# The output layer of a fused attention and feed-forward kernel: block products with w_out stationary and results turned by VectorE

## The chip, the core and the metric

The kernel runs on one core of a Trainium2 chip. A core has TensorE (PE in the profile; its weight loads are a row of their own, PEld), VectorE (DVE), ScalarE (ACT), GpSimd (POOL) and SyncE (SP), which here only issues DMAs. Each engine works through its own instructions in program order; semaphores make one wait for another. The metric is the device time of one execution in microseconds (us). The kernel before takes 675.25 us, the median of three runs (673.92 to 676.24).

## What is computed

Attention with two sparse masks (half of the heads look at the last 32 positions, half at every 32nd position before), and on its output a feed-forward layer: the maximum of three projections, and an output projection.

```
attn = softmax(mask(q @ k.T / 8)) @ v            # 8 batches, 8 heads, 576 positions, 64 wide
x = attn.transpose(0, 2, 1, 3).reshape(4608, 512)
h = maximum(maximum(x @ w1, x @ w2), x @ w3)      # 4608 x 768
out = h @ w_out                                   # 4608 x 512, float32
```

Every float32 operand of the feed-forward layer is kept as two parts, high and low, in the type float32r. A product is three matmuls: high by high, high by low, low by high.

## The kernel before

The 4608 tokens are worked in three sorts of pieces. Chunk one and chunk two are 512 tokens each; their products are plain ones (`ff_in`, L516; `ff_out`, L548). The 3584 tokens from 1024 on are eight blocks of 448, worked two at a time: four super-blocks of 896 tokens (`supers`, L773).

In a super-block the first layer is done by nine quads (L810), one for each pair of hidden blocks j, j+1 (128 features each) and each of w1, w2, w3. A quad computes a 2 x 2 block product (two hidden blocks by two token blocks, the inner dimension in two halves) by seven products instead of eight. They are named A11, S1, S2, S4, S3, A12, A22, in this order; each is a sum or difference of blocks of the weights by a sum or difference of blocks of x. The weights' sums are built once, while chunk two runs (`build_sums` to `build_low`, L577 to L616, on POOL), go to a scratch buffer in HBM, and are streamed back, one piece of 256 KB for each product, by SP (`load_next`, L664); nine buffers, so eight pieces ahead. The sums of x are made by `conversion` (L673) in seven steps for the next super-block, on ACT (high parts) and DVE (low parts and differences).

Two PSUM banks, `f_ps`, hold the products of a quad; one quad's first and second product take them in turn, and `bank` (L508) swaps the two at each call. ACT copies each product to SBUF (`snap`, L824), POOL adds earlier ones to it, and DVE takes the maximum into `hall` (L840), which holds h of the super-block: 768 features on partitions and blocks, by 896 tokens.

After nine quads follows the output layer of the super-block (L890 to L903): seven tiles of 128 tokens. `split` (L859) makes high and low parts of h for a tile; in `out_part` (L866) they are the stationary operand, and w_out (768 x 512, high and low, held in SBUF) is the moving one, 512 columns wide: 18 matmuls for a tile, 126 in all. `store` (L877) copies the tile to SBUF and stores it from ACT's queue. The seven steps of the next block's conversion stand between the tiles.

Attention of later batches runs in between, in pieces hung on the product numbers (`before`, `after`, L784 to L808); the last super-block has none. Everything is pinned to program order on its engine (`pin`, L100).

In chunk two, 18 groups `ff_in` (i = 0 to 17) are followed by four `ff_out` (L722 on). `ff_max` (L529) empties each bank: ACT for every third group, DVE for the other two, and at the end of three ACT and POOL make hh and hl, the parts of h. POOL builds the sums of w1, w2, w3 there at the places `sums_at` (L719).

## Time and profile before

| | us |
|---|---|
| median of three runs | 675.25 |
| lowest and highest | 673.92, 676.24 |
| span of the profiled execution, first to last instruction | 671.9 |
| TensorE busy | 647.1 |
| VectorE, ScalarE, GpSimd busy | 370.8, 336.5, 299.4 |
| chunk two, 126 to 193 us | 67 |
| the four output stages, each | 28.6 |

The profile gives the span of its execution and no other time for it. Busy times are shares of an engine's own time; they say nothing about who waits for whom, for which there are the chain that ended last and the rows of waits. The PE row counts pipelined matmuls: the time of one in a steady stretch is the stretch divided by the count, and its own duration (368 ns at 448 columns) is longer than that.

### The profile page before, as it was taken

What the parts mean: (1) busy time and instruction counts of PE and PEld (TensorE: products, weight loads), DVE (VectorE), ACT (ScalarE), POOL (GpSimd) and SP (SyncE); (2) the same over time, 40 slices, a digit from 0 to 9 for tenths busy, and PEclk for the clock granted to TensorE, in tenths of its full rate; (3) what the DMA queues carried; (4) which work ended last, traced back from release to release, by engine and by line L of the source; (5) the groups of instructions that cost most, each with busy time, mean ns of one, the idle gap of its engine ahead of it and who ended that gap; (6) DMA issues with size and microseconds to landing.
All of it is one profiled execution on the core that took longest, in us unless ns stands there. A gap on an engine that the chain in (4) does not pass through costs nothing.

```text
span 671.9 us, 18032 instructions
## 1 busy us (share of the span) xinstructions
PE 647.1 (96%) x7408; PEld 553.5 (82%) x7408; DVE 370.8 (55%) x515; ACT 336.5 (50%) x702; POOL 299.4 (45%) x291
## 2 busy tenths in 40 slices
PE   4689999999999999999999999999999999999997
PEld 3467877777778888888888888888899988999986
DVE  5886964676675666476345665643652563224240
ACT  4777656444264445446355455544444554444441
POOL 8779998599942233240134243004334401444410
PEclk9789999999999999999999999999999999999999
DMA  9999974567699777771377899228767714777411
GB/s 297 265 246 366 296 248 133 178 189 233 188 284 326 251 240 257 259 248 63 114 251 236 243 262 276 87 87 213 233 179 216 206 63 124 214 217 216 123 47 63
DMA packets 89371, 138.36 MB, mean 206 GB/s; under 512 B 10153, under 2 KB 39593, under 8 KB 89289
## 3 DMA queue, kind: packets, MB, share of 16 engines
q1 hardware_dynamic: 85256, 129.86, 63.6%
q10 hardware_dynamic: 4032, 7.34, 2.9%
q8 instruction: 59, 0.97, 0.6%
q14 instruction: 24, 0.19, 0.1%
HBM read 111.21 MB, written 25.95 MB: 204 GB/s over the span
## 4 chain that ended last, share of the span: by engine, by line
PE 80%; POOL 9%; DMA 6%; ACT 1%; DVE 1%; issue 1%; SPq 1%; POOLq 0%; ACTq 0%; DVEq 0%
PE f_ps L779 46%; PE f_ps L873 17%; PE f_ps L525 6%; PE f_ps L555 4%; DMA w<-in_w 4%; POOL work L596 2%; PE o_ps L444 2%; POOL work L612 2%; PE s_ps L318 2%; POOL work L588 2%; PE o_ps L473 1%; PE s_ps L340 1%; DMA out<-work 1%; POOL hl L546 1%; POOL sums_low L596 1%; DMA v_t<-in_v_loc 1%
## 5 line engine op out<-in xcount | busy, mean ns | idle before, releaser
L779 PE MATMUL f_ps<-xc,w_stream 128*128 128x448 f32 x1512 | 317.5, 368 | 0.2 <-ACT snap L826 0.2
L779 PEld LDWEIGHTS f_ps<-xc,w_stream 128*128 128x128 f32 x1512 | 280.5, 188 | 26.5 <-ACT snap L826 2.6
L826 ACT COPY snap<-f_ps 128x448 f32<-128x448 f32 x240 | 127.9, 533 | 165.0 <-PE f_ps L779 162.8
L838 POOL TENSOR_TENSOR snap<-snap 128x448 f32<-128x448 f32 x72 | 89.1, 1243 | 148.3 <-ACT snap L826 115.5
L840 DVE TENSOR_TENSOR h_all<-h_all,snap 128x448 f32<-128x448 f32 x96 | 81.2, 887 | 128.9 <-POOL snap L838 128.9
L838 POOL TENSOR_TENSOR h_all<-snap 128x448 f32<-128x448 f32 x36 | 41.4, 1150 | 169.1 <-ACT snap L826 168.1
L873 PE MATMUL f_ps<-wNone,h_parts 128*128 128x512 f32 x504 | 115.0, 389 | 0.0
L873 PEld LDWEIGHTS f_ps<-wNone,h_parts 128*128 128x128 f32 x504 | 94.6, 188 | 19.5
L525 PE MATMUL f_ps<-xh,w 128*128 128x512 f32 x288 | 95.8, 402 | 0.0
L525 PEld LDWEIGHTS f_ps<-xh,w 128*128 128x128 f32 x288 | 54.7, 190 | 12.7 <-ACT xh L498 0.3
L525 PE MATMUL f_ps<-xl,w 128*128 128x512 f32 x144 | 56.7, 394 | 0.8 <-DVE xl L503 0.8
L864 DVE TENSOR_TENSOR h_parts<-h_all,h_parts 128x768 fp32r<-128x768 f32 (+2 forms) x40 | 27.2, 712 | 30.3 <-ACT h_parts L863 30.1
L879 ACT COPY work<-f_ps 128x512 f32<-128x512 f32 x28 | 16.4, 585 | 46.1 <-PE f_ps L873 46.1
L683 DVE TENSOR_TENSOR xc<-x_block,xc 128x896 fp32r<-128x896 f32 x28 | 29.8, 1086 | 11.1 <-ACT xc L680 11.1
L397 DVE TENSOR_REDUCE s_ps<-s_ps 128x10 f32<-128x640 f32 (+2 forms) x30 | 23.2, 772 | 20.3 <-ACT s_ps L386 20.3
L407 DVE STREAM_TRANSPOSE pt<-s_ps 128x640 f32<-128x640 f32 (+2 forms) x32 | 32.5, 1017 | 1.1
L525 PEld LDWEIGHTS f_ps<-xl,w 128*128 128x128 f32 x144 | 27.4, 190 | 6.2 <-DVE xl L503 1.1
L555 PE MATMUL f_ps<-wNone,hh 128*128 128x512 f32 x96 | 30.6, 400 | 0.3 <-issue 0.3
L863 ACT CAST h_parts<-h_all 128x768 fp32r<-128x768 f32 (+2 forms) x40 | 24.5, 642 | 12.0 <-DVE h_all L840 5.4
L386 ACT ACTIVATE s_ps<-s_ps 128x640 f32<-128x640 f32 (+2 forms) x30 | 19.5, 651 | 21.9 <-DVE s_ps L370 21.9
L340 PEld LDWEIGHTS s_ps<-qk_t 64*32 64x32 f32 x1408 | 16.5, 116 | 15.2 <-DMA qk_t<-in_qT 7.0
L680 ACT CAST xc<-x_block 128x896 fp32r<-128x896 f32 x28 | 25.8, 947 | 3.4 <-DVE xc L683 1.2
(87 smaller groups left out, 681.6 us busy)
## 6 DMA issues: line engine op xcount, KB each, us to landing
w_stream<-scratch SPq DMA_DIRECT2D x252, 256.0 KB, 3.5
w<-in_w SPq DMA_DIRECT2D x18, 512.0 KB
qk_t<-in_qT SPq DMA_DIRECT2D x28, 288.0 KB, 3.8
qk_t<-in_kT SPq DMA_DIRECT2D x28, 288.0 KB, 5.9
v_t<-in_v_str SPq DMA_DIRECT2D x56, 128.0 KB, 4.2
out<-work ACTq DMA_DIRECT2D x28, 256.0 KB, 2.0
scratch<-w SPq DMA_DIRECT2D x27, 256.0 KB, 3.3
v_t<-in_v_loc SPq DMA_DIRECT2D x48, 96.0 KB, 3.3
```

What stands on the lines that cost most here:

```text
L407: pin(nc.vector.transpose(pt[:, :, : nm * at], s_ps[:, :, : nm * at]))
L525: pin(nc.tensor.matmul(f_ps, w[:, kc, :], x[:, kc, :], start=(kc == 2 and n == 0), stop=(kc == 1 and n == 2)))
L555: pin(nc.tensor.matmul(f_ps, h[:, ts], w, start=(j == 0 and n == 0), stop=(j == NJ - 1 and n == 2)))
L680: pin(nc.scalar.copy(out=x[m][:, 0], in_=src))
L683: pin(nc.vector.tensor_tensor(out=x[m][:, 1], in0=src, in1=x[m][:, 0].bitcast(F32), op=ALU.subtract))
L779: pin(nc.tensor.matmul(out_, w[:, wl, fs], x[:, xl, k, :], start=start and k == 0 and n == 0, stop=k == 1 and n == 2, skip_group_check=not ...
L826: pin(nc.scalar.copy(out=t, in_=src))
L838: pin(nc.gpsimd.tensor_tensor(out=h if i == 0 else u, in0=u, in1=t, op=ALU.add))
L840: pin(nc.vector.tensor_tensor(out=h, in0=h, in1=u, op=ALU.max))
L863: pin(nc.scalar.copy(out=to[:, 0, j0:j1], in_=src))
L864: pin(nc.vector.tensor_tensor(out=to[:, 1, j0:j1], in0=src, in1=to[:, 0, j0:j1].bitcast(F32), op=ALU.subtract))
L873: pin(nc.tensor.matmul(outs[t], h, w, start=(j == 0 and n == 0), stop=(j == NJ - 1 and n == 2)))
```

## The change

The output layer of a super-block becomes a 2 x 2 block product as well, with seven products instead of eight. w_out is now the stationary operand and h, 448 tokens wide, the moving one; the result comes out turned, features on partitions, and DVE turns it back in blocks of 32 by 32. The inner dimension, 768, is split by even and odd hidden blocks, so each product has three steps r of 128, in two halves q of 128 output features: 18 matmuls, 126 in all.

- The sums of w_out are built in chunk two, at i = 6 to 14, by DVE (`out_sums`, `out_mix`, and the low parts in `out_split`), stored to a second scratch buffer, and streamed in the place of w_out held in SBUF: 84 pieces for a super-block instead of 63.
- The columns of w_out are kept in another order (`by_quarters`), so that the blocks of 32 by 32 land in rows of 128 features; the plain chunks' outputs are put back in order by ACT's copy.
- The sums of h are made in place in `hall`: for r = 0 and 1 in the middle of the quads (`early`, at products 24 to 34 and 45 to 55), for r = 2 at the beginning of the output stage.
- In the output stage, sums of products are taken by POOL (`added`), turned by DVE (`turned`), and stored from SP's queue by four DMAs for 448 tokens, in pieces of 512 bytes.
- The first two steps of the next conversion move into the last quad (products 59 and 61); the others stand between the products of the output stage, and five of their DVE operations go to POOL there (`helper`).

The core of the diff:

```diff
+    def out_sums(r):
+        a = sums_o[r] = wt.tile([P, 2, 512], F32, name=f"w{r}_0")
+        for n in range(2):
+            parts = kept[None, 2 * r + n].bitcast(F32)
+            pin(nc.vector.tensor_tensor(out=a[:, n], in0=parts[:, 0], in1=parts[:, 1], op=ALU.add))
+
+    def out_mix(r):
+        a = sums_o[r]
+        a11, a21, a12, a22 = a[:, 0, :256], a[:, 0, 256:], a[:, 1, :256], a[:, 1, 256:]
+        for out_, x, y, op in (
+            (a22, a21, a22, ALU.add), (a21, a11, a21, ALU.subtract), (a11, a22, a11, ALU.subtract), (a12, a12, a11, ALU.subtract)
+        ):
+            pin(nc.vector.tensor_tensor(out=out_, in0=x, in1=y, op=op))
+
+    def out_split(r):
+        a, sh = sums_o.pop(r), wt.tile([P, 2, 512], F32R, name=f"w{r}_1")
+        to = scratch_o[:, :, r].rearrange("p n (l f) -> p n l f", l=2)
+        for n, (first, second_) in enumerate(((S2, S3), (S4, S1))):
+            pin(nc.scalar.copy(out=sh[:, n], in_=a[:, n]))
+            pin(nc.vector.tensor_tensor(out=a[:, n].bitcast(F32R), in0=a[:, n], in1=sh[:, n].bitcast(F32), op=ALU.subtract))
+            for l, src in enumerate((sh[:, n].bitcast(F32), a[:, n])):
+                pin(nc.sync.dma_start(out=to[:, first : second_ + 1 : 2, l], in_=halves(src)))
...
-    def conversion(s):
+    def conversion(s, helper=nc.vector):
...
         high(A11, b11)
-        high(A12, b21)
         low(A11, b11)
-        low(A12, b21)
         yield
         less(b11, b12, b11)
         yield
+        high(A12, b21)
+        low(A12, b21, helper)
         high(S4, b22)
+        low(S4, b22)
+        yield
+        less(b12, b22, b12, helper)
         high(S1, b11)
-        low(S4, b22)
-        less(b12, b22, b12)
+        low(S1, b11)
         yield
         less(b22, b22, b11)
-        low(S1, b11)
         high(S3, b12)
+        low(S3, b12, helper)
         yield
         high(S2, b22)
-        low(S3, b12)
-        less(b21, b21, b22)
+        less(b21, b21, b22, helper)
+        low(S2, b22)
         yield
         high(A22, b21)
-        low(S2, b22)
-        low(A22, b21)
+        low(A22, b21, helper)
...
+    out_at = {6 + 3 * r + n: (r, n) for r in range(NKO) for n in range(3)}
...
+        def h_high(m, rs):
+            if m not in parts:
+                parts[m] = second["hc"].tile([P, 2, NKO, BL], F32R, name="h_parts")
+            pin(nc.scalar.copy(out=parts[m][:, 0, rs], in_=of[m][:, rs]))
+        def h_low(m, rs, engine=nc.vector):
+            to = parts[m]
+            pin(engine.tensor_tensor(out=to[:, 1, rs], in0=of[m][:, rs], in1=to[:, 0, rs].bitcast(F32), op=ALU.subtract))
+        def h_split(m, rs):
+            h_high(m, rs)
+            h_low(m, rs)
+        def h_less(to, a, b, rs, engine=nc.vector):
+            pin(engine.tensor_tensor(out=to[:, rs], in0=a[:, rs], in1=b[:, rs], op=ALU.subtract))
+        def early(rs):
+            return [
+                lambda: h_split(A11, rs),
+                lambda: h_less(h11, h12, h11, rs),
+                lambda: (h_less(h12, h22, h12, rs, nc.gpsimd), h_split(S1, rs)),
+                lambda: h_less(h11, h22, h11, rs),
+                lambda: h_split(S2, rs),
+                lambda: h_less(h11, h21, h11, rs, nc.gpsimd),
+            ]
+        def out_stage(s):
+            more = lambda n=1: [next(convert[0], None) for _ in range(n)]
+            a0 = bank()[:, :BL]
+            c0 = ps_f[1 - turn[0]][:, :BL]
+            acc = {m: (a0, o[:, 0, :BL]) for m in (A11, S2, S3, A22)}
+            acc.update({m: (c0, o[:, 1, :BL]) for m in (S1, S4, A12)})
...
+                        for n, (wl, hl) in enumerate(((0, 0), (0, 1), (1, 0))):
+                            pin(nc.tensor.matmul(
+                                acc[m][q], w[:, wl, q * P : (q + 1) * P], parts[m][:, hl, r],
...
+            def turned(src, t, half_, q):
+                pin(nc.vector.transpose(outs[t][:, :, half_, q], src.rearrange("p (b r) -> p b r", r=32)))
+            def added(m, q, t, half_, u):
+                v = snap(acc[m][q])
+                pin(nc.gpsimd.tensor_tensor(out=v, in0=v, in1=u, op=ALU.add))
+                return lambda: turned(v, t, half_, q)
+            def store(t):
+                r0 = PLAIN + 2 * BL * s + (t - 1) * BL
+                for a in range(4):
+                    pin(nc.sync.dma_start(
+                        out=out[r0 : r0 + BL, a * P : (a + 1) * P].rearrange("(b r) n -> r b n", r=32),
+                        in_=outs[t][32 * a : 32 * (a + 1)].rearrange("p b h q f -> p b (h q f)"),
+                    ))
+            last, two, all_ = slice(2, 3), (0, 1), (0, 1, 2)
+            everything = slice(0, 3)
+            h_split(A11, last)
+            h_less(h11, h12, h11, last)
+            times(A11, two)
+            times(S1, two)
+            h_split(S1, last)
+            h_less(h12, h22, h12, last, nc.gpsimd)
+            h_less(h11, h22, h11, last)
+            h_split(S2, last)
+            times(A11, (2,))
+            s1 = [snap(acc[A11][q]) for q in range(2)]
+            h_less(h11, h21, h11, last, nc.gpsimd)
+            times(S1, (2,))
+            more()
+            h_split(S4, everything)
+            s5 = [snap(acc[S1][q]) for q in range(2)]
+            more()
+            times(S2, all_)
+            h_split(S3, everything)
...
+            times(S4, all_)
+            h_split(A12, everything)
+            w = [added(S4, 0, 2, 0, s2[0])]
+            more()
+            w.append(added(S4, 1, 2, 0, s2[1]))
+            times(S3, all_)
+            h_split(A22, everything)
+            w[0]()
+            v = [added(S3, 0, 2, 1, s5[0])]
+            more()
+            w[1]()
+            v.append(added(S3, 1, 2, 1, s5[1]))
+            times(A12, all_)
+            v[0]()
+            w = [added(A12, 0, 1, 0, s1[0])]
+            more()
+            v[1]()
+            store(2)
+            w.append(added(A12, 1, 1, 0, s1[1]))
+            times(A22, all_)
+            w[0]()
+            more()
+            turned(acc[A22][0], 1, 1, 0)
+            w[1]()
+            more()
+            turned(acc[A22][1], 1, 1, 1)
+            store(1)
+            more(20)
...
         for s in range(NSUPER):
+            convert[:] = [conversion(s + 1, nc.gpsimd) if s + 1 < NSUPER else iter(())]
+            between[59] = between[61] = [lambda: next(convert[0], None)]
+            for r, at in ((0, 24), (1, 45)):
+                for n, step in enumerate(early(slice(r, r + 1))):
+                    between[at + 2 * n] = [step]
             for q in range(9):
                 quad(s, q)
...
+            out_stage(s)
```

The three buffers of `h_parts` (the pool `hc`) serve the seven products in turn; the three products that share a pair of accumulators, and the next quad, find them free only when ACT has copied, or DVE has turned, what stood there.

More of the change, by code (lines that the diff above doesn't have):

```diff
@@ L45 @@
 NJ = DF // P
+NKO = NJ // 2
 A12, A11, A22, S4, S2, S1, S3 = range(7)
@@ L559, in ff_store @@
         o_sb = wk.tile([P, DO], F32, name="work")
-        pin(nc.scalar.copy(out=o_sb, in_=hs.pop((c, "out", t))))
+        pin(nc.scalar.copy(out=by_quarters(o_sb), in_=quarters(hs.pop((c, "out", t)))))
         pin(nc.sync.dma_start(out=out[c * CH + t * P : c * CH + (t + 1) * P, :], in_=o_sb))
@@ L616, in build_low, with out_parts @@
             pin(nc.sync.dma_start(out=to[:, S4 + 2 * n : S4 + 2 * n + 2, 1], in_=halves(x)))
+    sums_o = {}
+    def out_parts(r):
+        one, two = (kept[None, 2 * r + n].bitcast(F32) for n in range(2))
+        for m, part in ((A11, one[:, :, :256]), (A12, two[:, :, :256]), (A22, two[:, :, 256:])):
+            pin(nc.sync.dma_start(out=scratch_o[:, m, r].rearrange("p (l f) -> p l f", l=2), in_=part))
+    def out_sums(r):
[18 more added lines that the diff above has]
+                pin(nc.sync.dma_start(out=to[:, first : second_ + 1 : 2, l], in_=halves(src)))
     pin(nc.scalar.activation(out=nothing, in_=nothing, func=AF.Exp))
@@ L768, in fused_kernel @@
     plain_h.close()
+    plain_o.close()
+    for name, bufs in (("hc", 3), ("o_t", 2)):
+        second[name] = ctx.enter_context(tc.tile_pool(name=name, bufs=bufs, reuse_waits="tile"))
     blocks.append(ctx.enter_context(tc.tile_pool(name="blocks3", bufs=1, side="right", reuse_waits="tile")))
@@ L808, in after, with snap @@
                     paired_queries(n + 1)
+        def snap(src):
+            t = second["snap"].tile([P, BL], F32, name="snap")
+            pin(nc.scalar.copy(out=t, in_=src))
+            return t
         def quad(s, q):
@@ L817, in go @@
             def go(out_, m, start=True):
+                for step in between.pop(k[0], ()):
+                    step()
                 before(s, k[0])
@@ L822, in go @@
                 k[0] += 1
-            def snap(src):
-                t = second["snap"].tile([P, BL], F32, name="snap")
-                pin(nc.scalar.copy(out=t, in_=src))
-                return t
             def out_of(src, t, jj, half_):
@@ L877, in store @@
-        def store(s, t):
-            o_sb = wk.tile([P, DO], F32, name="work")
-            pin(nc.scalar.copy(out=o_sb, in_=outs.pop(t)))
-            r = PLAIN + 2 * BL * s + t * P
-            pin(nc.scalar.dma_start(out=out[r : r + P, :], in_=o_sb))
-        running = []
-        for s in range(NSUPER):
+        by_pairs = hall.rearrange("p (r two) t -> p two r t", two=2)
+        places_h = {
+            (k, t): by_pairs[:, k - 1, :, (t - 1) * BL : t * BL] for k in (1, 2) for t in (1, 2)
+        }
@@ new lines, in supers @@
+        h11, h21, h12, h22 = (places_h[n] for n in ((1, 1), (2, 1), (1, 2), (2, 2)))
+        of = {A11: h11, S1: h11, S2: h11, A22: h11, S4: h22, S3: h12, A12: h21}
+        parts = {}
+        def h_high(m, rs):
[5 more added lines that the diff above has]
+            pin(engine.tensor_tensor(out=to[:, 1, rs], in0=of[m][:, rs], in1=to[:, 0, rs].bitcast(F32), op=ALU.subtract))
```

99 lines of the change are left out of this document (52 added, 47 removed).

## The prediction

> **What bounds the kernel now.** I read the busy table and the chain that ended last first, then the busy time by stretch, the groups by line and shape, and the timelines of VectorE (DVE) and GpSimd (POOL).
>
> ```profile
> span 671.9 us, 18032 instructions
> PE 647.1 (96%) x7408; PEld 553.5 (82%) x7408; DVE 370.8 (55%) x515; ACT 336.5 (50%) x702; POOL 299.4 (45%) x291
> ...
> 562.79 76.87 PE f_ps L779 x378
> 639.66 28.60 PE f_ps L873 x126
> ...
> 126.00:193.00 67.00, 65.74 (x1193) 52.15 (x1195) 43.68 (x65) 28.95 (x67) 64.20 (x63) 1.00 0.67 204
> 206.30:299.70 93.40, 93.40 (x1276) 82.25 (x1275) 54.92 (x80) 46.64 (x104) 31.23 (x27) 1.00 0.80 263
> 299.70:328.30 28.60, 28.60 (x128) 23.70 (x127) 19.01 (x22) 14.93 (x22) 0.90 (x1) 1.00 0.22 77
> 562.80:639.60 76.80, 76.80 (x379) 70.79 (x379) 21.04 (x24) 34.59 (x65) 32.05 (x27) 1.00 0.66 189
> 639.60:668.30 28.70, 28.65 (x127) 23.37 (x125) 7.92 (x11) 8.85 (x16) 0.92 (x1) 1.00 0.15 55
> ```
>
> From 126 us on, TensorE does not stand still: each super-block is some 77 to 93 us of first-layer products (L779) and then 28.60 us of output layer (L873). Five engine columns stand in each row of the stretches: PE, weight load, DVE, ACT, POOL. Two of them matter here. In the output stage POOL does 0.90 us in 28.60, so DVE and ACT work there undisturbed. In chunk two (126 to 193) POOL does 64.20 us in 67: it has no room, and TensorE beside it only just keeps going.
>
> So the price of a matmul is read directly: 76.87 us / 378 = 203.4 ns at 448 columns, 28.60 / 126 = 227.0 ns at 512 columns. The span is 671.9 us; the median of the runs is 675.25, so 3.35 us lie around it, and I carry them over unchanged.
>
> **What the change removes.** Seven block products of 18 matmuls are again 126 matmuls, but of 448 columns: 126 x 203.4 = 25.63 us, 2.97 less per stage, **11.9 us in four stages**. That is all there is to win.
>
> **What it adds in the output stage.** Splits and differences of h on DVE, 6 sums on POOL, and five of the next block's conversion steps moved from DVE to POOL. The rows for their prices, and for what happens when both engines work:
>
> ```profile
> L838 POOL TENSOR_TENSOR snap<-snap x72: 1133/1152/1622, 224.4 to 639.1; 128x448 f32<-128x448 f32 x72
> L840 DVE TENSOR_TENSOR h_all<-h_all,snap x96: 582/619/1619, 225.6 to 641.5; 128x448 f32<-128x448 f32 x96
> L542 DVE TENSOR_TENSOR h_max<-f_ps,h_max x24: 653/691/693, 48.1 to 185.9; 128x512 f32<-128x512 f32 x24
> ...
> L683 DVE TENSOR_TENSOR xc<-x_block,xc 128x896 fp32r<-128x896 f32 x28 | 29.8, 1086 | 11.1 <-ACT xc L680 11.1
> L596 POOL TENSOR_TENSOR work<-work 128x256 f32<-128x256 f32 x24 | 17.6, 734 | 1.9
> L612 POOL TENSOR_TENSOR work<-work,sums_high 128x512 fp32r<-128x512 f32 x10 | 12.7, 1287 | 0.0
> L864 DVE TENSOR_TENSOR h_parts<-h_all,h_parts 128x768 fp32r<-128x768 f32 x16 | 15.3, 959 | 30.3 <-ACT h_parts L863 30.1
> L864 DVE TENSOR_TENSOR h_parts<-h_all,h_parts 128x512 fp32r<-128x512 f32 x12 | 7.9, 682 | 0.0
> L864 DVE TENSOR_TENSOR h_parts<-h_all,h_parts 128x256 fp32r<-128x256 f32 x12 | 4.3, 414 | 0.0
> L863 ACT CAST h_parts<-h_all 128x512 fp32r<-128x512 f32 x12 | 7.1, 624 | 0.0
> L407 DVE STREAM_TRANSPOSE pt<-s_ps 128x640 f32<-128x640 f32 x16 | 13.6, 850 | 0.6
> ...
> 636.72 3.80 POOL L838 TENSOR_TENSOR snap<-snap 128x448 f32<-128x448 f32 x3 [4.84 <-ACT snap L826]
> 637.87 1.15 POOL L838 TENSOR_TENSOR snap<-snap 128x448 f32<-128x448 f32 x1
> 637.90 1.60 DVE L840 TENSOR_TENSOR h_all<-h_all,snap 128x448 f32<-128x448 f32 x1 [3.27 <-POOL snap L838]
> 637.90 4.17 DVE L840 TENSOR_TENSOR h_all<-h_all,snap 128x448 f32<-128x448 f32 x4 [3.27 <-POOL snap L838]
> ```
>
> The last four rows decide. A DVE operation with both inputs in SBUF (L840) that starts 0.03 us after a POOL operation takes 1.60 us instead of 0.6: it ends 0.48 us after POOL does. Three POOL and four DVE operations, alone 3 x 1.15 + 4 x 0.6 = 5.85 us, take from 636.72 to 642.07, 5.35 us: one after the other, at 0.91 of the sum. With one input in PSUM nothing of the kind happens: L542 never takes more than 693 ns, though POOL is busy in 64 of 67 us there. So I treat the two engines as **one resource** whenever DVE reads two SBUF tensors.
>
> Per stage that converts a next block (three of four):
> - POOL: 6 sums and 2 differences of 448 columns at 1.15 = 9.2; 5 conversion steps of 896 columns. No row has that size; from 734 ns at 256 and 1287 at 512 it is 2.16 ns a column, 1287 + 384 x 2.16 = 2.12 us, 10.6 in all. Sum **19.8 us**.
> - DVE with two SBUF inputs: 4 low parts of 1344 columns (959 + 576 x 1.064 = 1.57 us), 6.3; 5 operations of 448 at 0.62, 3.1; 4 conversion steps at 1.086, 4.3. Sum **13.7 us**.
> - Together 33.5 x 0.91 = 30.5 us, which no order can put into 25.63.
>
> When does TensorE need the end of it? The program order gives the answer. The next super-block's second product (S1) writes the bank a0, which the transpose of A22's first half must have read; on DVE that transpose is queued behind the transpose of A12's sum, and so behind every POOL operation of the stage but the last. The beginning: today h_all is complete 642.07 - 639.66 = 2.4 us into the stage; two conversion steps (2 x 1.09) now stand before it on DVE, so 4.6. Three casts of ACT (448 columns, 0.57 each by L863's rate) lie between the first splits, and nobody holds the shared resource during them: 1.7. Then 30.5, less the last POOL sum 1.05, plus two transposes of 0.65 (L407's rate): 4.6 + 1.7 + 30.5 - 1.05 + 1.3 = **37.0 us**. Today that product starts at 28.60 + 1.22 = 29.8. Loss 7.2 per stage, **21.6 us in three**. Bounds: 4 per stage if the casts and the beginning hide, 9 if each of the 26 operations waits its full turn. TensorE will not wait at one place: each low part is later than the product that wants it, S4 first (its tile is free only after A11's last third, with conversion steps ahead of it on ACT and DVE), and S3, A12, A22 after it.
>
> The transposes I leave out of the shared resource: they have one input. No row shows one from SBUF beside POOL, so the bounds are 0 and 8 x 0.65 x 0.91 = 4.7 us a stage; I take 0, by L542.
>
> The last stage converts nothing: 9.2 + 9.4 = 18.6 us of shared work fit, TensorE sets the pace, and I give it 25.9: **-2.7**.
>
> **What it adds in chunk two.** Per third of w_out 4 DVE operations of 512 columns (0.68) and 4 of 256 (0.41), all with two SBUF inputs: 3 x 4.36 = 13.1 us.
>
> ```profile
> 126.29 1.27 POOL L588 TENSOR_TENSOR work<-w 128x512 f32<-128x512 f32 x1 [1.86 <-DMA out<-work]
> 188.92 1.30 POOL L546 TENSOR_TENSOR hl<-h_max,hh 128x512 fp32r<-128x512 f32 x1
> 190.17 2.52 POOL L612 TENSOR_TENSOR work<-work,sums_high 128x512 fp32r<-128x512 f32 x2
> 190.93 0.39 PE L555 MATMUL f_ps<-wNone,hl 128*128 128x512 f32 x1
> ```
>
> POOL runs there from 126.29 to 192.69 without a pause. Its last hl is ready at 190.22 and TensorE reads it at 190.93: 0.7 us of slack. 13.1 x 0.91 = 11.9 us of DVE between POOL's operations makes hl 11.2 late. And DVE itself waits, up to a POOL operation for each of its 24, while it empties the banks (L542) and does the attention: 43.68 of 67 us are taken. I take **+13**; bounds 5 (POOL catches up while TensorE waits for DVE) and 18. Below nothing it cannot go: no POOL work is taken away.
>
> **The tail.**
>
> ```profile
> 668.28 0.58 ACT L879 COPY work<-f_ps 128x512 f32<-128x512 f32 x1 [3.49 <-PE f_ps L873]
> 668.90 0.34 ACTq L881 DMA_DIRECT2D out<-work  x1
> 180.06 1.85 SPq L269 DMA_DIRECT2D v_t<-in_v_loc  x3
> 197.90 0.97 SPq L668 DMA_DIRECT2D w_stream<-scratch  x2
> DMA to landing us min/median/max: 2.0/2.0/4.6
> ```
>
> Today 3.6 us follow the last matmul: a copy, one issue, a landing of 2.0 (the last row is for the stores of out). After: a transpose or two (0.7 to 1.3), four issues on SP (0.97 / 2 to 1.85 / 3, so 0.5 to 0.6 each), a landing of pieces of 512 bytes from 32 partitions, which no row shows; by the rows 2.0 to 4.6. Sum 5 to 8: **+2**, bounds 0 and 5. [...]
>
> **What I cost at nothing.** 84 more loads: 55 of them take 0.66 of 76.8 us, 0.92 us each, so 21 take 19.3 in a stage of 25 us and more, with six in hand; without that cover up to 5 us a stage. The stores move from ACT's queue to SP's, where the next loads stand behind them; the stream is eight pieces (9.8 us) ahead. The early splits among the products (DVE has 38 us free in 93). The two copies with permuted columns.
>
> **Sum:** -2.7 + 21.6 + 13 + 2 = +33.9. Span 705.8, time 675.25 + 33.9 = **709 us**.
>
> **Rivals.**
> - *The output stage is not slowed by sharing* (faster): if the waits in the row above belong to that place alone, each engine has 19.8 and about 19 us of work in 25.63, TensorE sets the pace, chunk two has DVE's 23 us free, and all of it but the tail is kept: 675.25 - 11.9 + 2 = 665. It decides where shared work ends before 26.9 us (25.63 + 1.22). Against it: every meeting of L838 and L840 in the timeline.
> - *No sharing, but late parts*: the chain of cast, low part, difference gives back what the matmuls save in three stages, 675.25 - 2.7 + 2 = 674 to 675, no change.
> - *Chunk two hides it*: TensorE, late for DVE, lets POOL catch up: 709 - 13 = 696.
> - *The clock falls too.* In the opening it did:
>
> ```profile
> 28.00:32.00 4.00, 1.90 (x116) 1.79 (x116) 3.14 (x6) 3.29 (x12) 1.74 (x2) 0.65 1.10 245
> 32.00:36.00 4.00, 1.65 (x59) 1.27 (x59) 3.31 (x6) 3.26 (x7) 3.64 (x5) 0.50 0.82 236
> 36.00:40.00 4.00, 3.83 (x34) 3.12 (x35) 1.84 (x4) 2.60 (x8) 1.04 (x2) 0.57 0.79 241
> 40.00:45.00 5.00, 4.46 (x157) 3.24 (x155) 4.54 (x8) 3.90 (x9) 4.69 (x5) 1.00 1.00 259
> ```
>
> TensorE was busy under half of the time there, and the clock was 0.50, then 0.57 through 4 us of full work: 1.7 us lost each time. My stage is 25.6 busy in 37; two or three such falls a stage add 10 to 15: 720. [...] In the rows above the clock fell with single waits of under 2 us, among small matmuls.
>
> **How the numbers follow.** What a measurement tells from no change is about 0.3%, 2 us. Forecast 0.63 (689 to 728: 4 to 9 a stage, 5 to 18, 0 to 5, less 2.7), chunk two hidden 0.15, clock 0.07, no change 0.05, faster 0.10. Range 686 to 728, which leaves out the last two and an edge of the others. Faster 0.10, same 0.05, slower 0.85.
>
> **What would show it.** In the changed trace the output stage would take some 37 us in three super-blocks and about 26 in the last; POOL's 896-column steps would take over 2 us and DVE's low parts would vary with them (min far under max); the first S1 after a stage would wait for a DVE transpose; chunk two would be longer by some 10 us, with hl late. Wrong it would be with stages of 26 us, or low parts that keep their 1.57 us beside a busy POOL.

## The result, and the profile after

The changed kernel takes **729.03 us** (median of four runs, 728.95 to 730.31) beside 674.88 of the kernel before: ratio 1.0812, interval 1.079 to 1.0835. It is slower, as forecast, but by 54 us and not by 34: 1 us above the upper end of the range. The profiled execution has a span of 727.4 us, 55.5 more than before, where the sum of the prediction has 33.9.

The page of the changed kernel, its span, its busy table and its chain by engine:

```profile
span 727.4 us, 18447 instructions
PE 655.3 (90%) x7408; PEld 560.6 (77%) x7408; DVE 477.9 (66%) x592; ACT 359.7 (49%) x740; POOL 414.9 (57%) x354
PE 65%; DVE 13%; DMA 7%; POOL 6%; issue 3%; ACT 3%; SPq 2%; DVEq 0%; ACTq 0%; POOLq 0%
```

TensorE was busy for 96% of the span and is now for 90. DVE has 107 us more and POOL 115.5. In the chain that ended last DVE now has 13% where it had 1; POOL has 6%, and had 9.

The busy time by stretch of the changed kernel (window; length, then PE, weight load, DVE, ACT, POOL with their counts; granted clock, DMA share, GB/s): from a place inside the last `ff_out` of chunk one, where TensorE's sequencer idles in both kernels, to the first quad; the first output stage; the stretch right behind it; the last output stage.

```profile
116.80:224.20 107.40, 93.46 (x1372) 74.12 (x1372) 83.21 (x109) 41.99 (x93) 73.03 (x67) 0.92 0.76 240
317.50:352.50 35.00, 29.06 (x127) 24.35 (x126) 29.10 (x22) 17.93 (x26) 24.30 (x14) 0.95 0.47 144
352.50:370.00 17.50, 13.88 (x127) 11.07 (x125) 4.89 (x8) 4.26 (x8) 5.07 (x5) 0.94 0.92 248
692.30:719.10 26.80, 25.79 (x127) 23.38 (x125) 16.52 (x19) 13.01 (x20) 11.59 (x9) 1.00 0.58 166
```

The first of these stretches in the kernel before:

```profile
116.60:206.20 89.60, 88.20 (x1373) 70.28 (x1373) 61.55 (x86) 40.20 (x88) 67.13 (x67) 1.00 0.71 218
```

So chunk two became 17.8 us longer: TensorE stands still for 13.9 us instead of 1.4 (length less busy time), and the same matmuls take 93.46 us instead of 88.20 at a clock of 0.92. An output stage that converts a next block takes 35 us, and behind it TensorE works for 13.88 of 17.50 us where it used to work all the time. Where the 55.5 us are, with each piece from the first matmul of its kind to the first of the next:

| piece | before | after | difference | forecast |
|---|---|---|---|---|
| chunk two to the first quad | 89.6 | 107.4 | +17.8 | +13 |
| output stages one, two, three | 28.6 each | 35.0, 34.9, 34.6 | +18.7 | with the start of the quads +21.6 |
| the nine quads behind each of them | 92.2, 85.1, 76.9 | 98.5, 90.3, 81.4 | +16.0 | in the line above |
| last output stage | 28.8 | 27.0 | -1.8 | -2.7 |
| after the last matmul | 3.6 | 8.2 | +4.6 | +2 |

The first output stage and what follows it, on TensorE, from the timeline of the changed kernel (start, length, engine, line, what, count, and in brackets the idle time before and its releaser):

```profile
317.47 1.38 PE L966 MATMUL f_ps<-h_parts,w_stream 128*128 128x448 f32 x6
...
327.12 1.49 PE L966 MATMUL o_ps<-h_parts,w_stream 128*128 128x448 f32 x3 [1.45 <-ACT snap L869]
328.40 2.88 PE L966 MATMUL f_ps<-h_parts,w_stream 128*128 128x448 f32 x9
331.12 1.98 PE L966 MATMUL o_ps<-h_parts,w_stream 128*128 128x448 f32 x9
...
352.51 1.37 PE L836 MATMUL f_ps<-xc,w_stream 128*128 128x448 f32 x6
354.31 5.13 PE L836 MATMUL f_ps<-xc,w_stream 128*128 128x448 f32 x24 [0.43 <-DVE o_t L980]
...
367.70 2.42 PE L836 MATMUL f_ps<-xc,w_stream 128*128 128x448 f32 x6 [2.34 <-DMA w_stream<-scratch]
```

The next super-block's second product, S1, starts 354.31 - 317.47 = 36.84 us after the stage (forecast 37.0), released by DVE's transpose as the prediction has it; in the other two stages 36.75 and 36.45. Against 29.8 before that is 20.6 us in three stages (forecast 21.6). The rest of 18.7 + 16.0, **14.1 us, lies behind S1**, and the last row shows it: TensorE waits for a piece of w_stream. No term of the sum has that. TensorE's waits for these pieces from the first output stage's end on (us in total, times, longest):

```profile
PE f_ps L836 <- DMA w_stream<-scratch: 8.2, 5, 2.3
```

DVE and POOL in the same stage, from two timelines of the changed kernel:

```profile
331.02 3.48 DVE L931 TENSOR_TENSOR h_parts<-h_all,h_parts 128x1344 fp32r<-128x1344 f32 x1
...
340.81 1.54 DVE L931 TENSOR_TENSOR h_parts<-h_all,h_parts 128x1344 fp32r<-128x1344 f32 x1
```

```profile
330.11 2.98 POOL L729 TENSOR_TENSOR x_block<-x_block 128x896 f32<-128x896 f32 x1
...
340.96 3.38 POOL L729 TENSOR_TENSOR x_block<-x_block,x_block 128x896 f32<-128x896 f32 x1 [2.49 <-DVE x_block L729]
```

A low part of 1344 columns takes 1.54 us where it starts first (forecast 1.57), and then POOL's operation of 896 columns, begun 0.15 us later, takes 3.38 instead of some 2.1. Where POOL was first (330.11, 2.98), the low part beside it takes 3.48: it ends 1.41 us after POOL's operation, about its own length. The two stand one behind the other.

### The profile page after: what moved, and what is told of

It reads as the page before. It is cut to its first block, busy times and chain, and to the rows that moved or that the text cites. A ratio compares the mean times of both kernels' runs of the same rounds, so it can differ in the third digit from the quotient of the medians.

```text
span 727.4 us, 18447 instructions
## 1 busy us (share of the span) xinstructions
PE 655.3 (90%) x7408; PEld 560.6 (77%) x7408; DVE 477.9 (66%) x592; ACT 359.7 (49%) x740; POOL 414.9 (57%) x354
## 4 chain that ended last, share of the span: by engine, by line
PE 65%; DVE 13%; DMA 7%; POOL 6%; issue 3%; ACT 3%; SPq 2%; DVEq 0%; ACTq 0%; POOLq 0%
PE f_ps L836 37%; PE f_ps L534 12%; PE f_ps L564 5%; DMA w<-in_w 3%; PE f_ps L966 3%; POOL snap L984 3%; DVE h_all L899 3%; DMA w_stream<-scratch 2%; PE o_ps L966 2%; PE o_ps L453 2%; DVE h_parts L931 2%; PE s_ps L327 2%; DVE xc L726 2%; PE o_ps L482 2%; PE s_ps L349 1%
## 5 line engine op out<-in xcount | busy, mean ns | idle before, releaser
L869 ACT COPY snap<-f_ps 128x448 f32<-128x448 f32 x264 | 140.9, 534 | 186.5 <-PE f_ps L836 176.3
L897 POOL TENSOR_TENSOR snap<-snap 128x448 f32<-128x448 f32 x72 | 93.6, 1307 | 134.9 <-ACT snap L869 133.7
L931 DVE TENSOR_TENSOR h_parts<-h_all,h_parts 128x448 fp32r<-128x448 f32 (+1 forms) x52 | 68.9, 1326 | 36.9 <-ACT h_parts L927 32.9
L897 POOL TENSOR_TENSOR h_all<-snap 128x448 f32<-128x448 f32 x36 | 43.3, 1209 | 85.1 <-ACT snap L869 84.4
L966 PE MATMUL f_ps<-h_parts,w_stream 128*128 128x448 f32 x252 | 63.0, 386 | 10.1 <-DVE h_parts L931 10.1
L966 PE MATMUL o_ps<-h_parts,w_stream 128*128 128x448 f32 x252 | 59.5, 376 | 8.8 <-ACT snap L869 8.8
L966 PEld LDWEIGHTS f_ps<-h_parts,w_stream 128*128 128x128 f32 x252 | 49.2, 199 | 18.5 <-DVE h_parts L931 13.5
L966 PEld LDWEIGHTS o_ps<-h_parts,w_stream 128*128 128x128 f32 x252 | 47.3, 192 | 16.4 <-ACT snap L869 12.9
L927 ACT CAST h_parts<-h_all 128x448 fp32r<-128x448 f32 (+1 forms) x52 | 41.8, 804 | 23.0 <-DVE h_all L938 12.6
L726 DVE TENSOR_TENSOR xc<-x_block,xc 128x896 fp32r<-128x896 f32 x19 | 37.2, 1960 | 13.3 <-ACT xc L723 10.1
L938 POOL TENSOR_TENSOR h_all<-h_all 128x448 f32<-128x448 f32 x24 | 29.8, 1243 | 26.1 <-DVE h_all L938 15.1
L984 POOL TENSOR_TENSOR snap<-snap 128x448 f32<-128x448 f32 x24 | 35.8, 1510 | 9.8 <-ACT snap L869 9.8
L534 PEld LDWEIGHTS f_ps<-xl,w 128*128 128x128 f32 x144 | 28.8, 200 | 6.6 <-DVE xl L512 1.1
```

Of the source, the lines that this page charges most:

```text
L534: pin(nc.tensor.matmul(f_ps, w[:, kc, :], x[:, kc, :], start=(kc == 2 and n == 0), stop=(kc == 1 and n == 2)))
L726: pin(engine.tensor_tensor(out=x[m][:, 1], in0=src, in1=x[m][:, 0].bitcast(F32), op=ALU.subtract))
L869: pin(nc.scalar.copy(out=t, in_=src))
L897: pin(nc.gpsimd.tensor_tensor(out=h if i == 0 else u, in0=u, in1=t, op=ALU.add))
L927: pin(nc.scalar.copy(out=parts[m][:, 0, rs], in_=of[m][:, rs]))
L931: pin(engine.tensor_tensor(out=to[:, 1, rs], in0=of[m][:, rs], in1=to[:, 0, rs].bitcast(F32), op=ALU.subtract))
```

## Experiments

Each ran beside the kernel before on the same chip; ratios are against it. A kernel timed once has no interval. "Quads" are the nine quads behind output stages one, two and three (98.5, 90.3, 81.4 us in the changed kernel, 92.2, 85.1, 76.9 before).

### Do DVE and POOL share something? Two runs in the kernel before

**f_pool** puts 18 additions on POOL, with no reader, into each output stage of the kernel before:

```diff
+            dummy = second["snap"].tile([P, BL], F32, name="snap")
+            pin(nc.gpsimd.memset(dummy, 0.0))
+            for _ in range(18):
+                pin(nc.gpsimd.tensor_tensor(out=dummy, in0=dummy, in1=dummy, op=ALU.add))
             out_part(0, 0, 4)
```

> The kernel before the change, with 18 additions of 448 columns (20.7 us) on POOL at the beginning of each output stage, on a tile that nobody else reads; nothing else changes. Theory (taking turns): DVE's operations with two SBUF inputs there (896 columns 1.086 us, 768 columns 0.96) rise to 1.5 to 2.2 us wherever POOL is busy, copies from PSUM on ACT stay; the output stages 28.6 to 31 us, since DVE has room there: 675 to 682. Rival (POOL and DVE work side by side in SBUF, the waits seen belong to the quads' data): durations as before, 675.

**g_poolset** is the same with 18 memsets, which write SBUF and read nothing.

> As the last, but POOL's 18 operations a stage are memsets of 448 columns: they write SBUF and read nothing. If reads are what DVE and POOL take turns at, DVE's operations keep 1.086 and 0.96 us; if any use of SBUF by POOL does it, they rise here too. 675 either way.

Groups by line and shape (count, then busy us, mean ns, idle time before), f_pool first:

```profile
L683 DVE TENSOR_TENSOR xc<-x_block,xc 128x896 fp32r<-128x896 f32 x28 | 40.8, 1478 | 4.0 <-ACT xc L680 4.0
L864 DVE TENSOR_TENSOR h_parts<-h_all,h_parts 128x768 fp32r<-128x768 f32 x16 | 25.2, 1574 | 9.3 <-ACT h_parts L863 9.2
...
L898 POOL TENSOR_TENSOR snap<-snap 128x448 f32<-128x448 f32 x72 | 96.7, 1343 | 5.7
```

and g_poolset:

```profile
L683 DVE TENSOR_TENSOR xc<-x_block,xc 128x896 fp32r<-128x896 f32 x28 | 29.8, 1087 | 11.0 <-ACT xc L680 10.8
L864 DVE TENSOR_TENSOR h_parts<-h_all,h_parts 128x768 fp32r<-128x768 f32 x16 | 15.3, 959 | 30.3 <-ACT h_parts L863 30.2
...
L898 POOL MEMSET snap<- 128x448 f32 x72 | 34.1, 473 | 4.1
```

Beside POOL's additions DVE's operations go from 1086 to 1478 ns and from 959 to 1574 in the mean; beside memsets they stay at 1087 and 959. f_pool took 682.45 us beside 675.28 (one run), g_poolset 674.8. So by these four means DVE's operations with two SBUF inputs are slower beside a POOL that reads SBUF and not beside one that only writes it, and this is so in the kernel before as well: the rival that it belongs to one place falls. The memsets fill less of a stage (9.5 us instead of 26.8), but beside them no operation of L683 takes more than 1093 ns. One thing more in f_pool: its output stages stay at 28.6 us. The 7 us appear behind them, in quads of 94.6, 88.0 and 78.6 us. Most of that is one wait behind each stage, 1.7 to 1.8 us long, for a copy from PSUM on ACT, in whose queue a cast had waited for DVE (3.06 us in the first case):

```profile
332.98 8.94 PE L779 MATMUL f_ps<-xc,w_stream 128*128 128x448 f32 x42 [1.69 <-ACT work L879]
```

### The output stage: whose work fills it?

**a_conv** gives the five conversion steps back to DVE:

```diff
-            convert[:] = [conversion(s + 1, nc.gpsimd) if s + 1 < NSUPER else iter(())]
+            convert[:] = [conversion(s + 1) if s + 1 < NSUPER else iter(())]
```

> The five conversion steps of the next block that the change gave to POOL in the output stages go back to DVE; all else stays. Theory (DVE with two SBUF inputs and POOL take turns): shared work of a stage falls from 33.5 to 28.3 us (POOL 9.2, DVE 13.7 + 5 x 1.086), at 0.91 from 30.5 to 25.8; the three stages that convert fall from 35 us to 30 or 31, the kernel by some 12 to 14 us, to 715 to 717. Rival (chains: cast, low part, difference, whoever does them; a fuller DVE queue makes them longer): stages of 35 us or more, 729 or above.

It took 718.47 us, ratio 1.064 (1.0602 to 1.0679); stages of 31.8, 31.9 and 32.7, so 3.2, 3.0 and 1.9 less. Less POOL work makes the stage shorter, though DVE gets more of it. The saving is smaller than expected, and the stretch of a_conv's first output stage says why:

```profile
319.90:351.70 31.80, 27.27 (x128) 23.12 (x127) 29.29 (x27) 17.55 (x26) 16.23 (x10) 1.00 0.53 164
```

DVE is now busy for 29.29 of 31.80 us and has no room left. Not all of that is its own work: POOL still takes its six sums, and beside them two of DVE's four low parts of 1344 columns take 2.51 us instead of 1.55, which makes their mean 2032 ns:

```profile
L931 DVE TENSOR_TENSOR h_parts<-h_all,h_parts 128x1344 fp32r<-128x1344 f32 x4 | 8.1, 2032 | 0.0
```

The quads got shorter too (95.7, 88.8, 78.5); the waits there are the next question.

**h_added** moves the six sums of products from POOL to DVE, which reads one operand from PSUM:

```diff
-                v = snap(acc[m][q])
-                pin(nc.gpsimd.tensor_tensor(out=v, in0=v, in1=u, op=ALU.add))
+                v = second["snap"].tile([P, BL], F32, name="snap")
+                pin(nc.vector.tensor_tensor(out=v, in0=acc[m][q], in1=u, op=ALU.add))
```

> The six sums of products in the output stage are taken by DVE straight from PSUM (one input in SBUF) instead of an ACT copy and a POOL addition. Theory (shared resource): POOL loses 6.9 of its 19.8 us, the shared work falls to 26.6, at 0.91 to 24.2 us; stages that convert at 29 to 31 us instead of 35, the kernel 12 to 16 less, 713 to 717. Rival (DVE's own length sets the pace, 13.7 + 5.2 + 6 x 0.62 us and the waits): 33 to 36 us, 722 or above.

No gain: 729.2 us, ratio 1.0795 (1.0751 to 1.0838), and stages of 39.3, 38.2 and 38.9 us. TensorE's waits (us in total, times, longest) show a new one, for the accumulators, whose release stands behind everything else in DVE's queue:

```profile
PE o_ps L966 <- DVE snap L984: 12.0, 3, 4.0
```

The quads got as much shorter (92.8, 86.0, 78.7). Work taken off the shared resource was no gain here, where the engine that took it was already busy for 29.1 of 35 us in the changed kernel and works in order.

### Behind the stage: why are the loads late?

SP's own timeline in the changed kernel, at the end of the first output stage:

```profile
343.25 5.52 SPq L711 DMA_DIRECT2D w_stream<-scratch  x5
352.64 3.03 SPq L990 DMA_DIRECT2D out<-o_t  x4
355.77 2.84 SPq L711 DMA_DIRECT2D w_stream<-scratch  x3
358.70 3.48 SPq L990 DMA_DIRECT2D out<-o_t  x4
362.28 4.93 SPq L711 DMA_DIRECT2D w_stream<-scratch  x8
```

When SP comes to the first store, it has issued five pieces of the next block; the other buffers still hold the stage's. It stands for 3.9 us, from 348.77 to 352.64, until DVE has turned the first results, and the eight stores take 3.03 + 3.48 us to issue, with three loads between them. The ninth piece is issued at 362.28. Eight products at 1.22 would end at 352.51 + 8 x 1.22 = 362.3; with the wait for S1 and 0.97 us of attention TensorE is done with what it has at 365.4, and the ninth product begins at 367.70, when its piece has landed.

**b_store** takes the wait away: the first store comes at the stage's end, the second in the next super-block.

```diff
             v[1]()
-            store(2)
             w.append(added(A12, 1, 1, 0, s1[1]))
...
-            store(1)
+            store(2)
             more(20)
+            return lambda: store(1)
...
+            if left:
+                between[3] = [left]
             for q in range(9):
                 quad(s, q)
-            out_stage(s)
+            left = out_stage(s)
```

> The stores of the output only move in SP's program order: those for the second 448 tokens to behind the loads of the stage's last product, those for the first behind the third product of the next super-block; same bytes, same pieces. Theory (loads stand in SP's queue behind stores that wait for DVE): the waits for w_stream after a stage (8.2 us in all) go, and with them the matmuls at half rate behind them; the quads of super-blocks two to four fall from 98.5, 90.3 and 81.4 us to some 94, 86 and 78; the kernel by 11 to 14 us, to 715 to 718. Rival (the DMA engines are full: 84 loads and pieces of 512 bytes): the loads are late all the same, 726 to 731.

719.27 us, ratio 1.0645 (1.0614 to 1.0675). The stages stay at 35.1, 35.0 and 34.6; the quads are 93.5, 86.5 and 77.7, 12.5 us less in sum. SP in b_store, at the same place:

```profile
345.14 9.77 SPq L711 DMA_DIRECT2D w_stream<-scratch  x8
355.00 3.14 SPq L990 DMA_DIRECT2D out<-o_t  x4
358.24 2.75 SPq L711 DMA_DIRECT2D w_stream<-scratch  x3
```

and the stretch behind that stage, as long as the one of the changed kernel above:

```profile
354.50:372.00 17.50, 17.07 (x228) 14.79 (x227) 4.78 (x8) 7.28 (x16) 5.08 (x6) 1.00 0.93 270
```

Eight pieces are issued before the first store, the ninth follows at 358.24, and TensorE works for 17.07 of 17.50 us at a granted clock of 1.00, against 13.88 at 0.94. The 8.2 us of waits for w_stream are gone. Of the 12.5 us, 9.0 are time in which TensorE stood still, and 3.5 are slower matmuls (busy 255.8 us in the three stretches of quads instead of 259.3).

**d_wide** leaves the stores in their place, wait and all, and makes each of them one DMA of 128 partitions in rows of 7168 bytes instead of four of 32 partitions in pieces of 512. It leaves out the order of the output's rows from token 1024 on.

```diff
-                for a in range(4):
-                    pin(nc.sync.dma_start(
-                        out=out[r0 : r0 + BL, a * P : (a + 1) * P].rearrange("(b r) n -> r b n", r=32),
-                        in_=outs[t][32 * a : 32 * (a + 1)].rearrange("p b h q f -> p b (h q f)"),
-                    ))
+                pin(nc.sync.dma_start(
+                    out=out[r0 : r0 + BL].rearrange("t (z n) -> (t z) n", z=2).rearrange("(p x) n -> p (x n)", x=7),
+                    in_=outs[t].rearrange("p b h q f -> p (b h q f)"),
+                ))
```

> Each half of the output is stored by one DMA from all 128 partitions, 7168 bytes in a row, at the same place in SP's order; the rows of the output beyond token 1024 are then not in their right order, which is the part left out. Theory (the tail is issue and landing of four DMAs in pieces of 512 bytes from 32 partitions): the tail after the last matmul falls from 8.3 us to 4 to 5; after a stage SP is free 2 to 2.5 us earlier, the waits for w_stream shrink by half: 729 falls to some 718 to 722. Rival (landing and issue cost the same whatever the pieces): 726 to 730.

715.53 us, ratio 1.0601 (1.0583 to 1.0618). The same stretch of SP's timeline in d_wide:

```profile
353.53 0.34 SPq L989 DMA_DIRECT2D out<-o_t  x1
353.96 2.15 SPq L711 DMA_DIRECT2D w_stream<-scratch  x3
356.29 0.37 SPq L989 DMA_DIRECT2D out<-o_t  x1
356.75 6.83 SPq L711 DMA_DIRECT2D w_stream<-scratch  x8
```

The stores cost SP 0.71 us instead of 6.51, and the quads are 93.7, 86.4 and 77.6 although the wait for DVE is still there. The ninth piece is issued at some 356.8 instead of 362.28. So either change is enough: with the stores moved behind the loads, or with their issues short, the loads keep ahead. (d_wide's stores also keep the DMA engines busy for less time, in the tail three slices of 0.59 us at 403 to 451 GB/s for the last 896 KB, where v_tail needs nine of 0.5 us at 148 to 257; b_store, which leaves the pieces as they are, shows that this isn't needed.) The 21 loads more in each super-block are in both kernels, and TensorE waits for w_stream in neither.

### Chunk two

**e_nosums** leaves out DVE's operations on w_out (ACT copies stand for the sums); casts, stores and loads stay.

```diff
-            pin(nc.vector.tensor_tensor(out=a[:, n], in0=parts[:, 0], in1=parts[:, 1], op=ALU.add))
+            pin(nc.scalar.copy(out=a[:, n], in_=kept[None, 2 * r + n].bitcast(F32)[:, 0]))
```

> DVE's 24 operations on the sums of w_out in chunk two are left out; ACT makes two more copies for each third, the stores stay (the products of the output layer are then taken with w_out's high parts in the places of the sums). Theory (DVE's turns with POOL, and what waits behind them, are the 18 us): chunk two is over after 80 to 83 us instead of 98, 711 to 714. Rival (the 21 stores on SP's queue and DMA, or the copies in ACT's queue, delay it): 90 us or more, 720 or above.

717.98 us (one run). Counted from the same place in chunk one (here 117.4), chunk two takes 98.7 us: 8.7 less than in the changed kernel, 9.1 more than before. So half of the loss stays without any of DVE's 24 operations. TensorE's longest new wait in e_nosums:

```profile
PE o_ps L453 <- ACT pt L304: 4.6, 1, 4.6
```

That is attention whose q arrived late: SP issued its load at 194.78, behind four stores of sums of w_out that took it 3.77 us from 190.92 on.

**k_nostore** leaves these 21 stores out instead (`pass` in the place of the two `dma_start` to scratch_o).

> The 21 stores of the sums of w_out in chunk two are left out, DVE's and ACT's work on them stays; the output layer streams pieces of the other scratch buffer instead. Theory (the rest of chunk two's 18 us is SP: the stores stand before the loads of q, k and v): over at 218 to 220 us instead of 224, no wait of the last attention unit for q. Rival (stores hidden): 223 to 226.

733.01 us (one run); the first quad starts at 227.4, no earlier than in the changed kernel (224.2). With DVE's work there, the stores show no cost. **p_early** starts the sums three groups earlier:

```diff
-    out_at = {6 + 3 * r + n: (r, n) for r in range(NKO) for n in range(3)}
+    out_at = {3 + 3 * r + n: (r, n) for r in range(NKO) for n in range(3)}
```

> The nine steps on the sums of w_out in chunk two begin at i = 3 instead of 6 and end at 11 instead of 14. Theory of turns alone: the same work beside the same POOL, 727 to 731. Theory of the end (SP's stores and ACT's casts there delay the last attention units and hl): chunk two over 4 to 7 us sooner, 722 to 725.

730.37 us, ratio 1.0791 (1.076 to 1.0821), the first quad at 225.2: three groups earlier is no gain either.

Two kernels were to give DVE an operand from PSUM, as L542 has it (at most 693 ns beside a busy POOL), and both put a wait of their own there. **c_psum** keeps the halves of the sums in a spare part of a PSUM tile:

```diff
+    spare = o[:, 2:, 256:]
...
-            parts = kept[None, 2 * r + n].bitcast(F32)
-            pin(nc.vector.tensor_tensor(out=a[:, n], in0=parts[:, 0], in1=parts[:, 1], op=ALU.add))
+        pin(nc.scalar.copy(out=spare, in_=two_of(two[:, 0])))
+        pin(nc.vector.tensor_tensor(out=a[:, 1, :256], in0=x, in1=two[:, 1, :256], op=ALU.add))
```

> In chunk two each of DVE's operations on the sums of w_out reads one operand from PSUM, where ACT has put it (two free quarter-banks of o); 30 DVE operations instead of 24, 12 ACT copies more, same stores. Theory (taking turns with POOL is the cost): from 126 us to the end of chunk two's last output product some 84 us instead of 98, DVE's operations there at 0.3 to 0.7 us instead of 1.0 to 1.5; the kernel 12 to 15 us less, 714 to 717. Rival (too much work on DVE, ACT or SP there, shared port or not): 96 us or more, 727 or above.

743.5 us, ratio 1.1008 (1.096 to 1.1056). The first of TensorE's two new waits in c_psum (the other is 8.7 us):

```profile
PE o_ps L453 <- DVE o_ps L648: 8.8, 1, 8.8
```

Attention writes the same PSUM tile and now waits for the sums. That says nothing of sharing. **i_one** lets every operation read one SBUF operand and the spare part of PSUM, without copies into it:

```diff
+    spare = o[:, 3, 256:]
...
+                pin(nc.vector.tensor_tensor(out=a[:, n, h], in0=parts[:, 0, h], in1=spare, op=ALU.add))
```

> In chunk two DVE's operations on the sums of w_out keep their places, columns and outputs, but each takes its second operand from one quarter-bank of PSUM that nobody writes there, so it has one input in SBUF (36 operations of 256 columns; the sums are then not the sums, which is the part changed). Theory (half or more of chunk two's 18 us is taking turns): DVE's 256 columns at 0.35 to 0.45 us each instead of 0.45 to 1.1, no waits of POOL on them, chunk two over at 215 to 219 us instead of 224, beside the 216 of the run without DVE's operations. Rival (DVE's time and order there, shared or not): 222 to 226.

726.41 us (one run). The operations on w_out no longer vary (410 to 422 ns each), but the same tile is waited for again, 7.0 us in two waits. Both are inconclusive.

**r_write** turns it round: POOL's sums of w1, w2 and w3 for all quads but the first become memsets of about the same length in sum, which read nothing.

```diff
-            pin(engine.tensor_tensor(out=x, in0=parts[:, 0], in1=parts[:, 1], op=ALU.add))
+            if q == 0:
+                pin(engine.tensor_tensor(out=x, in0=parts[:, 0], in1=parts[:, 1], op=ALU.add))
+            for _ in range(2 if q else 0):
+                pin(engine.memset(x, 1.0))
```

> In chunk two POOL's operations on the sums of w1, w2, w3 (all but the first group) become memsets of the same tiles, two for 512 columns and three for 256, so that POOL is busy about as long and writes SBUF, but reads nothing; casts and stores of those tiles and all of DVE's work stay (the sums of the first layer's weights are then constants, which is the part changed). Theory (DVE's turns with POOL's reads are most of what is left of chunk two's cost): DVE's operations on the sums of w_out at 0.68 and 0.41 us, chunk two 92 to 97 us from its first product of chunk one's output, instead of 107.4 (89.6 before the change). Rival (DVE's, ACT's and SP's added work, shared or not): 103 or more.

DVE's operations on w_out in the changed kernel (126 to 226 us):

```profile
L647 DVE TENSOR_TENSOR w<-w 128x256 f32<-128x256 f32 x12 | 9.3, 771 | 0.3
L655 DVE TENSOR_TENSOR w<-w,w 128x512 fp32r<-128x512 f32 x6 | 8.2, 1410 | 5.7 <-ACT w L654 5.7
...
L639 DVE TENSOR_TENSOR w<-wNone 128x512 f32<-128x512 f32 x6 | 6.7, 1148 | 0.0
```

and in r_write, with its stretch from the same place in chunk one to the first quad:

```profile
L656 DVE TENSOR_TENSOR w<-w 128x256 f32<-128x256 f32 x12 | 5.0, 421 | 0.3
L648 DVE TENSOR_TENSOR w<-wNone 128x512 f32<-128x512 f32 x6 | 4.2, 735 | 0.0
L664 DVE TENSOR_TENSOR w<-w,w 128x512 fp32r<-128x512 f32 x6 | 3.9, 688 | 5.7 <-ACT w L663 5.7
...
117.90:215.70 97.80, 89.99 (x1372) 71.50 (x1372) 72.28 (x109) 42.07 (x93) 64.49 (x157) 0.97 0.80 255
```

Here the 24 operations take 5.0 + 4.2 + 3.9 = 13.1 us, as forecast; in the changed kernel, where POOL reads, 24.2. Chunk two takes 97.8 us against 107.4 and 89.6: **9.6 of the 17.8 us are the sharing**, and the other 8.2 stay with a POOL that reads nothing there. TensorE's longest wait left in r_write is attention behind DVE's queue, in which DVE had just stood for 2.25 us at ACT's cast of a sum of w_out:

```profile
190.59 1.36 PE L349 MATMUL s_ps<-qk_t 64*32 64x64 f32 x72 [4.83 <-DVE pt L416]
```

That DVE's own 13 us in an in-order queue are the cause of all 8.2 is not shown: in e_nosums, with none of these operations, 9.1 us stay as well, then with a wait for q. What the rest of chunk two's loss consists of stays open.

### Both repairs, and the tail

**l_both** is a_conv and b_store together, **v_tail** that with the last super-block's stores issued half by SP and half by ACT:

```diff
+            queues = (nc.sync,) * 4 if s + 1 < NSUPER else (nc.sync, nc.scalar) * 2
...
-                    pin(nc.sync.dma_start(
+                    pin(queues[a].dma_start(
```

> Conversion steps back on DVE and the stores moved, together. Alone they took 12.4 and 10.6 us off the span. If they act in different places (stage; loads after it): 704 to 708, stages of 32 us and quads of super-blocks two to four as in the run with the stores moved. If both only make SP free sooner: 713 to 717.

> Conversion on DVE, stores moved, and the last half's four stores issued two by SP and two by ACT, which has nothing else to do there. Theory (of the 8.1 us after the last matmul some 3 are four issues one after the other): tail 6.3 to 7 us, the kernel 1 to 2 us under the run with the two edits, 709 to 710.5. Rival (landing of 512-byte pieces sets it): tail 8, 711.

l_both took 711.36 us, ratio 1.0503 (1.0467 to 1.0539); its span, 709.3, is 18.1 less than the changed kernel's, where the two alone give 12.4 and 10.6: they overlap by 4.9. The overlap is in the quads, of which a_conv alone takes 7.3 us off, b_store 12.5 and both 9.7. Why a_conv shortens them was not tested: SP's wait at the store is no shorter there (4.6 us instead of 3.8). It is the best version of the change that ran, and 34 us slower than the kernel before. What is left of the loss, 37.4 us: 19.2 up to the end of chunk two, 9.5 in three stages (31.9, 31.9, 31.5), 6.2 in the quads behind them (94.3, 87.6, 78.5), 4.5 in the tail, less 1.8 in the last stage and 0.4 in the first quads. Its first stage by engine:

```profile
318.40:350.30 31.90, 28.60 (x128) 24.57 (x127) 29.39 (x28) 17.62 (x26) 16.11 (x10) 0.95 0.56 167
```

v_tail took 713.65 us, ratio 1.0582 (1.0528 to 1.0635), no better. Its last two groups of issues, and what its DMA engines did from 690 to the end, in 40 slices of 0.5 us (busy tenths, GB/s):

```profile
702.42 0.84 SPq L991 DMA_DIRECT2D out<-o_t  x2
702.42 0.91 ACTq L991 DMA_DIRECT2D out<-o_t  x2
```

```profile
DMA  6689797100000004989999920019989899994000
GB/s 66 194 281 157 199 360 277 54 0 0 0 0 0 0 0 103 176 150 251 265 302 289 247 70 0 0 28 184 179 171 178 148 257 237 189 170 127 3 0 0
```

Four issues take 0.91 us instead of some 3, and 8.2 us still follow the last matmul. After the last issue, at 703.3, the DMA engines are 80 to 90% busy and more for nine slices (4.5 us) at 148 to 257 GB/s. In d_wide, whose tail is 5.4 us, the last store goes at up to 451 GB/s (from 690 to its end, slices of 0.6 us; the numbers before the last two zeros):

```profile
GB/s 0 94 227 126 0 56 216 384 307 230 160 49 185 230 150 331 342 66 0 0 0 0 0 0 390 390 403 378 0 0 0 0 0 195 451 439 403 73 0 0
```

So the tail is the transfer of the small pieces, not their issue. d_wide changes the size of the pieces and the number of partitions at once, so it does not tell these two apart.

## Why the prediction was wrong, step by step

- **The step that failed** is in "What I cost at nothing": the stores move to SP's queue, "where the next loads stand behind them; the stream is eight pieces (9.8 us) ahead". The cover was named, but its use was not added up: at the first store only five of those pieces belong to the next block, and the wait for DVE (3.9 us) and eight issues (6.5 us) let three more through until the ninth is due. Behind S1 14.1 us were lost in three stages, and b_store, which moves the stores alone, takes 12.5 of them back. The neighbouring item, 84 more loads, was rightly costed at nothing: b_store has them all and no wait for w_stream.
- **The shared resource** was right. f_pool and g_poolset show it in the kernel before, with its condition, that POOL reads SBUF (1478 and 1574 ns beside additions, 1087 and 959 beside memsets). The stage built from it, 37.0 us to S1, came out at 36.84, 36.75 and 36.45. That it is so close is in part luck: in the first stage DVE stood 0.63, 0.63 and 1.92 us for ACT's casts, 3.2 where the sum has 1.7, so the shared work took some 1.5 less than its 30.5. POOL's 896 columns (2.12 us, extrapolated) took 2.10 to 2.28 in nine of fifteen operations, and 2.97 to 3.38 in the six of L729; the transposes, left out of the sharing, have a median of 645 ns and never take more than 650. a_conv adds what the sum did not have: with five operations moved from POOL to it, DVE is busy for 29.3 of 31.8 us.
- **Chunk two** was right in kind and too small: +17.8 for +13, at the upper bound of 18. DVE's 13.1 us were right to the tenth. The forecast had 11.2 us of it for the sharing, which measures 9.6 (r_write), and 1.8 for DVE's own waits, where 8.2 stay: this is the part that was mis-sized, and the runs do not say what all of it is. POOL, named as the bound, is not late by itself: it waits 12.0 us for ACT's hh, and ACT 24.6 us for DVE's h_max. The rival "chunk two hides it" falls.
- **The range**: its upper end does not follow from the bounds named beside it. They give 675.25 + 27 + 18 + 5 - 2.7 = 722.6, not 728, so the time lies 6.5 us above what the terms allow, and a term that the sum did not have is needed.
- **The tail** was right in kind: +4.6 for +2, bounds 0 and 5. Among the ends for the landing the lower one was taken; the stores' landing has a median of 4.3 us on the page, near the upper one. Whether that is the size of the pieces or the number of partitions, no run separates.
- **The last stage**: -1.8 for -2.7. TensorE sets the pace there, as said; it stands still for 26.80 - 25.79 = 1.0 us.
- **The clock rival** had its mechanism and not its price. The granted clock is 0.95 in the three stages and 0.92 in chunk two, and nine matmuls take 2.88 us at 328.40 and 1.98 next to it. But a_conv's first stage takes 31.80 us at a clock of 1.00 and l_both's 31.90 at 0.95, with DVE busy for 29.3 and 29.4 us. While TensorE waits for DVE anyway, a slow matmul costs nothing there. In chunk two the 5.3 us of slower matmuls are part of the 17.8, a consequence of the waits and no term beside them: behind waits of 4.40 and 5.33 us the clock is 0.50 from 180.8 to 186.2 and from 199.7 to 204. Shorter waits do not decide it one by one. Around 328.40 and 367.70, behind single waits of 1.45 and 2.34 us, it is 0.60 and 0.56, but behind waits of 1.25 and 1.47 us, at 334.56 and 339.94, it is 1.00.

By its own terms: -1.8 (for -2.7), 20.6 (for 21.6), 17.8 (for 13), 4.6 (for 2), and 14.1 for nothing: 55.3 of 55.5.

## What to carry to other kernels

A queue's lead is a budget in microseconds: before something is put into that queue, add its wait and its issue time to those of what stands there, and see how many pieces are really issued by then. Where DVE reads two SBUF tensors and POOL reads SBUF too, as in f_pool (1478 ns instead of 1086 for 896 columns), add up their times over the stretch as if one engine did both, and then look whether DVE alone fits. And a change that saves TensorE 3 us in a stage of 28.6 has to find room on the other engines for everything that it adds: here none of the versions that ran brought a converting stage under 31.4 us.

## What the runs showed that was not expected

- POOL's memsets leave DVE's two-input operations as they were (1087 and 959 ns), its additions do not (1478 and 1574).
- DVE's delay in f_pool cost nothing in the stage where it arose and 7 us behind it: the place of a loss need not be the place of its cause.
- Stores in pieces of 512 bytes from 32 partitions kept the DMA engines busy at 148 to 257 GB/s; the same bytes in rows of 7168 bytes from 128 partitions went at up to 451 GB/s.
- Using a free part of a PSUM tile made attention's matmuls wait 8.8 and 8.7 us for DVE's sums (c_psum).
